# A 1x1 depthwise and pointwise convolution: GpSimd synchronises the critical section, and the start of the kernel is laid out differently

## The chip, the cores and the metric

The kernel runs on one core of one Trainium2 chip. The time is in device microseconds (us) of that core, the median of several executions. One execution was also taken by the hardware profiler; its span and its trace are what the views below come from.

## What is computed

The reference, cut to what matters (k is 1, so the padding is nothing and the loop has one turn):

```python
def reference(x, dw, pw):            # x (1,384,384,384), dw (1,1,384), pw (384,384), bf16
    out = zeros_like(x)
    for i in range(k):
        for j in range(k):
            out = out + xp[:, i:i+H, j:j+W, :] * dw[i, j][None, None, None, :]
    return jnp.einsum('bhwc,cd->bhwd', out, pw)
```

Each of 147,456 pixels has 384 channels. They are scaled by dw, one factor per channel, and multiplied with the 384 x 384 matrix pw. The kernel folds the scaling into the weights: out = x @ (diag(dw) @ pw).

## The kernel before, in words

**Tiling.** 512 pixels make a supertile, and there are 288 of them (NS). A supertile lies in SBUF as 128 partitions of 4 pixels each. The pixels are loaded in chunks of 1, 1, 2, 2, 4 supertiles (group 0), then of 10, and in smaller ones at the end; `load_x` (L111) issues a chunk's load and `store` (L126) its store, both on SyncE's queue. The order of loads and stores on SyncE is a list sorted by due times (L157 to L167): the loads of groups 0 to 2 come first, each later load waits until the group that had its buffer has been transposed.

**The main loop.** VectorE (DVE) transposes each supertile in two halves (`transposes`, L284): 32 x 32 blocks of 32-bit words, that is of channel pairs, from X to T. TensorE (PE) then makes 48 matmuls per supertile (`supertile`, L180): twelve steps (b, par), where b is a block of 64 channels and par tells even from odd channels, times four row groups q of 32 rows that run side by side, one PSUM bank each. ScalarE (ACT) copies the finished supertile from PSUM to the output buffer O (L347). PE's loop holds two supertiles (s = 0, 1), with one PSUM tile each, and its waits are in the loop's body: for the transposes (`s_t`, steps 0 and 6), for ScalarE's copy of the supertile before (`s_a`), and, for s = 0 alone, for the weights (`s_wr`, `w_first`, L178, steps 0, 8 and 10).

**The weights.** Each row group needs the weights of its own 32 rows, scaled by dw. They are made on PE itself (`w_copy`, L207): a selection matrix `sel_w`, which holds dw's factors, times the rows of pw, gives the scaled rows repeated for the four row groups, in PSUM. From there ScalarE and VectorE copy them to `w_r` (`w_out`, L304), in six pieces, five on ScalarE. `sel_w` comes from an identity matrix `eye` that GpSimd makes (L272), reduced by VectorE to `sel` (L312), and from `dw_f`, a column of dw that PE turns out of a row by four tiny matmuls (L240).

**The order at the start.** ScalarE's queue issues dw (L146) and the second piece of pw, 64 rows of 1,536 bytes (L151). SyncE's queue issues the first piece of pw, 128 rows of 1,536 bytes (L147), then x0 (L155), x1, and so on up to the two loads of 10 supertiles. PE fills the time with `idle_work` (L223): rounds of four matmuls on a constant tile of ones that is there before the kernel's own code starts; four rounds ahead of the dw matmuls, three behind them, all written out. Then it waits for the first piece of pw (`s_pw`), makes pieces 0, 1, 2, waits for the second piece of pw (`s_pe0`), and makes the others in pairs of 32-row tiles, with some repeats.

**The critical section.** All of this stands in one critical section (L102), in which the kernel sets its own semaphores. One engine, SyncE by default, signals to all others that it begins and collects them at its end.

The functions that the change touches:

## Time and profile before

| | us |
|---|---|
| median of 3 runs | 577.86 (577.42 to 578.03) |
| the profiled execution's own time | 577.42 |
| its span | 575.70 |
| PE busy | 568.3 (99%) |
| DVE busy | 507.7 (88%) |
| ACT busy | 419.4 (73%) |
| DMA | 226.88 MB, 394 GB/s over the span |

The span is the stretch from the first to the last instruction of the profiled execution; the time of that execution is 1.72 us longer. PE's busy time is that of matmuls, which overlap in the array, so the pace is better read from how many start in a stretch than from the busy share. L188 is the line of the main loop's matmuls, L212 that of the weight copies, L226 that of the idle work, L294 that of the transposes.

### The profile page before, as it was taken

What the parts mean: (1) busy time and instruction counts of PE and PEld (TensorE: products, weight loads), DVE (VectorE), ACT (ScalarE), POOL (GpSimd) and SP (SyncE); (2) the same over time, 40 slices, a digit from 0 to 9 for tenths busy, and PEclk for the clock granted to TensorE, in tenths of its full rate; (3) what the DMA queues carried; (4) which work ended last, traced back from release to release, by engine and by line L of the source; (5) the groups of instructions that cost most, each with busy time, mean ns of one, the idle gap of its engine ahead of it and who ended that gap; (6) DMA issues with size and microseconds to landing.
All of it is one profiled execution on the core that took longest, in us unless ns stands there. A gap on an engine that the chain in (4) does not pass through costs nothing.

```text
span 575.7 us, 29720 instructions
## 1 busy us (share of the span) xinstructions
PE 568.3 (99%) x13876; PEld 383.9 (67%) x13876; DVE 507.7 (88%) x586; ACT 419.4 (73%) x297; POOL 0.5 (0%) x5
## 2 busy tenths in 40 slices
PE   8999999999999999999999999999999999999996
PEld 4666666666666666666666666666666666666664
DVE  6888898889888988899888988898889888988894
ACT  5777777777777777777777777777777777777775
POOL 0000000000000000000000000000000000000000
PEclk9999999999999999999999999999999999999999
DMA  8999999999999999999999999999999999999676
GB/s 326 432 360 428 420 424 434 432 432 411 387 430 390 394 400 429 392 390 402 419 398 392 402 416 409 390 405 418 406 406 426 395 393 394 421 396 374 265 289 236
DMA packets 25220, 226.88 MB, mean 394 GB/s; under 512 B 1209, under 2 KB 5242, under 8 KB 21370
## 3 DMA queue, kind: packets, MB, share of 16 engines
q1 hardware_dynamic: 24096, 225.91, 97.1%
q10 hardware_dynamic: 1114, 0.89, 0.5%
q14 instruction: 9, 0.07, 0.0%
q8 instruction: 1, 0.02, 0.0%
HBM read 113.54 MB, written 113.25 MB: 394 GB/s over the span
## 4 chain that ended last, share of the span: by engine, by line
PE 98%; DMA 1%; DVE 0%; ACTq 0%; issue 0%; DVEq 0%; SPq 0%
PE ps L188 98%; DMA pw_n<-in_pw_dram 1%; PE ps L212 0%; DVE O L345 0%; ACTq L146 0%; ACTq L380 0%; DVEq L341 0%; SPq L102 0%
## 5 line engine op out<-in xcount | busy, mean ns | idle before, releaser
L188 PE MATMUL ps<-w_r,T 32*128 32x384 bf16 x13824 | 562.8, 321 | 0.0
L294 DVE STREAM_TRANSPOSE T<-X 128x384 uint32<-128x384 uint32 x572 | 500.9, 876 | 57.9 <-DMA X<-in_x_dram 1.6
L347 ACT CAST O<-ps 128x1536 bf16<-128x1536 f32 x287 | 413.1, 1439 | 147.7 <-PE ps L188 147.7
L188 PEld LDWEIGHTS ps<-w_r,T 32*128 32x128 bf16 x13824 | 381.7, 93 | 181.4 <-issue 0.7
L307 ACT CAST w_r<-ps 128x768 bf16<-128x768 f32 x5 | 3.8, 801 | 2.3 <-PE ps L212 2.1
L212 PE MATMUL ps<-pw_n,sel_w 32*128 32x384 bf16 x20 | 2.9, 517 | 1.6 <-DMA pw_n<-in_pw_dram 1.6
L294 DVE STREAM_TRANSPOSE T<-Xl 128x384 uint32<-128x384 uint32 x4 | 3.5, 877 | 0.4
L345 DVE CAST O<-ps 128x384 bf16<-128x384 f32 x2 | 1.0, 552 | 3.1 <-PE ps L188 3.1
L226 PE MATMUL ps<-const-bfloat16-1.0 32*128 32x384 bf16 x28 | 2.6, 515 | 1.1 <-SPq L102 1.1
L212 PEld LDWEIGHTS ps<-pw_n,sel_w 32*128 32x128 bf16 x20 | 1.0, 124 | 3.3 <-DMA pw_n<-in_pw_dram 2.6
L282 ACT ACT_TABLE_LOAD x1 | 1.3, 1283 | 2.1 <-issue 2.1
L226 PEld LDWEIGHTS ps<-const-bfloat16-1.0 32*128 32x128 bf16 x28 | 0.7, 123 | 1.6 <-issue 1.6
L312 DVE TENSOR_REDUCE sel<-eye 128x32 f32<-128x128 bf16 x1 | 0.4, 367 | 1.4 <-POOL eye L272 1.4
L307 DVE CAST w_r<-ps 128x768 bf16<-128x768 f32 x1 | 1.0, 958 | 0.7 <-PE ps L212 0.7
L344 ACT CAST O<-ps 128x384 bf16<-128x384 f32 x2 | 0.9, 482 | 0.5 <-PE ps L188 0.5
L319 DVE COPY dw_f<-ps 128x2 f32<-128x2 f32 x1 | 0.2, 160 | 1.0 <-PE ps L240 1.0
L325 DVE TENSOR_SCALAR sel_w<-sel,dw_f 128x128 bf16<-128x128 f32 (+1 forms) x4 | 0.9, 278 | 0.0
L240 PEld LDWEIGHTS ps<-const-bfloat16-1.0,dw_row 1*128 1x128 bf16 (+1 forms) x4 | 0.4, 130 | 0.4 <-DMA dw_row<-in_dw_dram 0.4
L240 PE MATMUL ps<-const-bfloat16-1.0,dw_row 1*128 1x1 bf16 (+1 forms) x4 | 0.4, 191 | 0.0
L272 POOL TENSOR_SCALAR_AFFINE_SELECT eye<-const-bfloat16-1.0 128x128 bf16<-128x128 bf16 x1 | 0.3, 295 | 0.6 <-SPq L102 0.6
L282 ACT COPY warm<-const-float32-0.0 128x1 f32<-128x1 f32 x2 | 0.3, 190 | 0.0
L320 DVE COPY dw_f<-ps 64x2 f32<-64x2 f32 x1 | 0.1, 142 | 0.0
(4 smaller groups left out, 0.4 us busy)
## 6 DMA issues: line engine op xcount, KB each, us to landing
X<-in_x_dram SPq DMA_DIRECT2D x26, 3840.0 KB, 21.4
out_dram<-O SPq DMA_DIRECT2D x26, 3840.0 KB, 27.1
X<-in_x_dram SPq DMA_DIRECT2D x3, 1536.0 KB, 17.6
out_dram<-O SPq DMA_DIRECT2D x3, 1536.0 KB, 7.5
X<-in_x_dram SPq DMA_DIRECT2D x3, 768.0 KB, 9.0
out_dram<-O SPq DMA_DIRECT2D x3, 768.0 KB, 11.2
X<-in_x_dram SPq DMA_DIRECT2D x1, 2304.0 KB, 19.3
out_dram<-O SPq DMA_DIRECT2D x1, 2304.0 KB, 11.1
```

What stands on the lines that cost most here:

```text
L188: mm = nc.tensor.matmul(PS[s][:, q, :D], lhsT=Ts[s][32 * q : 32 * q + 32, b, par::2], rhs=w_r[32 * q : 32 * q + 32, b, par, :], start=n == ...
L212: mm = nc.tensor.matmul(ps[:, at + k, :D], lhsT=sel_w[row : row + 32, slot, :, :].rearrange("p q w -> p (q w)"), rhs=pw_n[row : row + 32, ...
L226: nc.tensor.matmul(PS[i // 2][:, i - 2 if i > 1 else 2 + i, :D], lhsT=ones[32 * i : 32 * i + 32, 0:P], rhs=ones[32 * i : 32 * i + 32, :], ...
L240: mm = nc.tensor.matmul(PS[0][0:m, 0, D + k : D + k + 1], lhsT=dw_row[:, c0 : c0 + 2 * m - 1 : 2], rhs=ones[0:1, 0:1], start=True, stop=Tr ...
L282: nc.scalar.copy(warm[:, s : s + 1], nc.const_aps.tensor(0.0, [P, 1], F32)).then_inc(s_a[s])
L294: ins = nc.vector.transpose(out=Tw[:, 3 * h : 3 * h + 3], in_=Xw[:, :, j, 96 * h : 96 * h + 96].rearrange("p k (b w) -> p b k w", w=32),)
L307: o = nc.scalar.copy(out, in_) if e else nc.vector.tensor_copy(out, in_)
L312: nc.vector.tensor_reduce(out=sel[:], in_=eye[:].rearrange("p (u j) -> p j u", j=32), op=mybir.AluOpType.add, axis=mybir.AxisListType.X,). ...
L325: nc.vector.tensor_scalar_mul(sel_w[0:m, k], sel[0:m].unsqueeze(1).to_broadcast([m, 4, 32]), dw_f[0:m, k : k + 1]).then_inc(s_sw)
L344: nc.scalar.copy(Ov[:, q, j, :], PS[s][:, q, :D]).then_inc(s_a[s])
L345: nc.vector.tensor_copy(Ov[:, q + 1, j, :], PS[s][:, q + 1, :D]).then_inc(s_d)
L347: a = nc.scalar.copy(Ov[:, :, j, :], PS[s][:, :, :D])
```

## The change

The critical section is synchronised by GpSimd instead of SyncE, and GpSimd's drain is left out. The rest of the difference lies in the start:

- pw is one load on SyncE's queue, three rows of 768 bytes per partition, where it was two loads on two queues. x0 is issued on ScalarE's queue, behind dw; SyncE's second DMA is then x1.
- `ones` is no longer a constant that is there at the start. GpSimd makes `warm`, `zero` and `ones` by memsets, then `eye`. PE's idle work uses `zero`, waits for it, and is two loops of three rounds.
- dw is turned by three matmuls into three columns; `sel` has 64 columns and `sel_w` is made by three multiplications of 256 columns, where it was four of 128.
- The weight copies are made in pairs of 64-row tiles, in the order of their blocks, 18 matmuls for 20.
- The main loop's first eight steps go through par first and b second: (0,0), (0,1), (1,0) ... where it was (0,0), (1,0), (0,1), (1,1), (2,0), (2,1), (3,0), (3,1). The last four are as before.

```diff
-    ones = nc.const_aps.tensor(1.0, [P, D], BF16)
-    with tc.tile_critical():
+    with tc.tile_critical(sync_engine=mybir.EngineType.Pool, no_gpsimd_drain=True):
...
         nc.scalar.dma_start(dw_row[:], dw.rearrange("a e c -> a (e c)")).then_inc(s_dw, 16)
-        nc.sync.dma_start(
-            pw_n[:, 0:2].rearrange("p t d -> p (t d)"),
-            pw[0 : 2 * P, :].rearrange("(p t) d -> p (t d)", t=2),
-        ).then_inc(s_pw, 16)
-        nc.scalar.dma_start(
-            pw_n[0:64, 2:4].rearrange("p t d -> p (t d)"),
-            pw[2 * P : C, :].rearrange("(p t) d -> p (t d)", t=2),
-        ).then_inc(s_pe0, 16)
-        load_x(0)
+        load_x(0, nc.scalar)
+        nc.sync.dma_start(pw_n[:], pw.rearrange("(k p) d -> p k d", p=P)).then_inc(s_pw, 16)
...
-        steps = [(0, 0), (1, 0), (0, 1), (1, 1), (2, 0), (2, 1)]
-        steps += [(3, 0), (3, 1), (4, 0), (5, 0), (4, 1), (5, 1)]
-        w_first = {0: [(0, 1), (1, 3)], 8: [(1, 4)], 10: [(1, 5)]}
+        w_eng = [1, 0, 1, 1, 1, 1]
+        w_done = [(s_wr[e], w_eng[: i + 1].count(e)) for i, e in enumerate(w_eng)]
+        w_first = {(0, 0): [(0, 1), (1, 3)], (4, 0): [(1, 4)], (4, 1): [(1, 5)]}
+        steps = [(b, par) for b in range(4) for par in range(2)] + [(4, 0), (5, 0), (4, 1), (5, 1)]
...
         def idle_work(n):
-            for _ in range(n):
+            with nc.tensor.Fori(0, n, 1) as _:
                 for i in range(4):
                     nc.tensor.matmul(
-                        PS[i // 2][:, i - 2 if i > 1 else 2 + i, :D],
-                        lhsT=ones[32 * i : 32 * i + 32, 0:P],
-                        rhs=ones[32 * i : 32 * i + 32, :],
+                        PS[0][:, i, :D],
+                        lhsT=zero[32 * i : 32 * i + 32, 0:P],
+                        rhs=zero[32 * i : 32 * i + 32, :],
...
-        idle_work(4)
+        nc.tensor.wait_ge(s_zero, 1)
+        idle_work(3)
+        nc.tensor.wait_ge(s_seed, 2)
         nc.tensor.wait_ge(s_dw, 16)
-        for k in range(4):
+        for k in range(3):
...
         idle_work(3)
         nc.tensor.wait_ge(s_pw, 16)
...
+        times = {(1, 1): 3, (2, 0): 2}
+        for k in range(3):
+            nc.tensor.wait_ge(s_sw, k + 1)
+            for r in range(2):
+                if k == 2:
+                    nc.tensor.wait_ge(*w_done[r])
+                for v in [0, 1] * times.get((k, r), 1):
+                    mm = nc.tensor.matmul(
+                        PS[(k + 1) % 2][:, 2 * r + v, :D],
+                        lhsT=sel_w[64 * v : 64 * v + 64, k, r, :, :].rearrange("p q w -> p (q w)"),
+                        rhs=pw_n[64 * v : 64 * v + 64, k, :],
...
+                mm.then_inc(s_w)
...
+        nc.gpsimd.memset(warm[:], 0.0).then_inc(s_seed)
+        nc.gpsimd.memset(zero[:].bitcast(U32), 0).then_inc(s_zero)
+        nc.gpsimd.memset(ones[:], 1.0).then_inc(s_seed)
         nc.gpsimd.affine_select(
             out=eye[:],
-            in_=ones[:, 0:P],
+            in_=ones[:],
...
+        )._wait_ge(s_seed, 2).then_inc(s_sel)
...
-        for k in range(4):
+        for k in range(3):
             nc.vector.tensor_scalar_mul(
-                sel_w[0:m, k], sel[0:m].unsqueeze(1).to_broadcast([m, 4, 32]), dw_f[0:m, k : k + 1]
+                sel_w[:, k], sel[:].unsqueeze(2).to_broadcast([P, 2, 4, 32]), dw_f[:, k : k + 1]
             ).then_inc(s_sw)
```

## The prediction

> **What bounds the kernel now.** I read the profile in this order: the chain that ended last, the pace of the main loop's matmuls, the waits of the first microseconds, the landings of the loads. The chain, in order of time (start us, length us, what):

> ```profile
> 1.53 4.52 DMA pw_n<-in_pw_dram
> 6.06 0.05 issue
> 6.10 2.10 PE ps L212 x14
> 8.20 0.04 issue
> 8.25 562.85 PE ps L188 x13824
> ```

> From 8.25 us TensorE (PE) never waits again, and what follows the main loop is 4.6 us (575.70 - 571.10). So the change can act in three places: the pace of the loop, the 8.25 us ahead of it, the 4.6 us behind it. First the pace. The rows below are the main loop's instructions alone in three stretches of 2 us; the (x) behind PE is how many matmuls started:

> ```profile
> 8.25:10.25 2.00, 2.00 (x28) 1.16 (x32) 1.00 1.06 433
> 10.50:12.50 2.00, 2.00 (x56) 1.37 (x52) 1.00 1.02 436
> 100.00:102.00 2.00, 2.00 (x56) 1.37 (x52) 1.00 0.94 399
> ```

> The first 2 us go at half pace, though the granted clock beside them reads 1.00. In the steady part one supertile takes 1.95 us (ScalarE's copies of finished supertiles start at 11.47, 13.42, 15.37 us); 288 x 1.95 = 561.6, and the other 1.25 us are the 1.0 us lost in the half-pace stretch and the last matmul's drain. I therefore count with an effective start: loop start plus half of the slow stretch, now 8.25 + 1.0 = 9.25.

> What holds 8.25? The second piece of pw, issued third after dw and x0: it lands 4.5 us after its issue, and PE waits 1.6 us for it, then makes the last weight copies. The x loads behave alike. Here are the landings of the first x load, of the second with VectorE's wait for it, and of the one for supertiles 10 to 19 (each from the answer for that DMA alone, issued at 1.46, 1.93 and 3.83 us):

> ```profile
> DMA to landing us min/median/max: 3.2/3.2/3.2
> ...
> who waited for it (us, times):
>   DVE T L294: 1.2, 1
> ...
> DMA to landing us min/median/max: 6.2/6.2/6.2
> ...
> DMA to landing us min/median/max: 22.4/22.4/22.4
> ```

> So x0 is there at 4.7, x1 at 8.1, the large one at 26.2 us. DMA is busy from 2 us on (slices 2 to 8: 252, 369, 293, 235, 320, 381 GB/s), so each byte put ahead of x0 delays it.

> **The change, part by part.**

> *Main loop: 0.* The (b, par) order of the first eight steps changes; the waits sit at the same steps (0, 6, 8, 10) and the count of matmuls is the same. The half with four orderly steps and the half with mixed ones run at one pace now (56 matmuls per 2 us), so I take 0.

> *GpSimd as synchronising engine: -0.1.* At the start all engines are let go at 0.79 to 0.88 us by SyncE's signal; GpSimd's would come within 0.05 us of that. At the end SyncE now signals 574.6, collects four engines and signals again, up to the span's end at 575.7. GpSimd must still collect SyncE's own end. I cost the 1.1 us at -0.1, between -0.4 (one of the hand-overs gone) and +0.3 (GpSimd polls more slowly). GpSimd's drain alone is too short to matter: the 1.1 us hold some ten such steps.

> *GpSimd's memsets: +0.4 for PE's first matmul.* Now constants laid down before the start feed PE at 1.12. After, three memsets and the affine_select follow the start one by one. Rows: MEMSET of one column 0.10 us, affine_select of 128 columns 0.295. The zero tile (192 words) lies between 0.10 and 0.45; I take 0.3, nearer to the wider row: PE starts near 1.5, and the eye is ready near 2.1 instead of 1.4. VectorE's reduction (0.37) ends near 2.5, still ahead of the dw column, which is needed near 2.9, so it costs nothing.

> *Weights ready: 7.05 instead of 8.25.* PE: first idle block, 3 rounds at 0.32 = 0.96, to 2.45 (dw is there at 2.30); dw matmuls 0.36 as now (2.37 to 2.73); second block 0.96: 3.8, and 0.1 for the two small loops' branches (between 0, as the main loop shows none, and 0.4): 3.9. VectorE beside it: dw_f at 2.9, 0.16 later the first sel_w. One sel_w of 128 columns takes 0.28 us, four 0.87; with 256 columns each 0.28 to 0.45, so ready near 3.6, 3.9, 4.3, ahead of their use. pw as one load on SyncE's queue with nothing ahead: 192 KB landed 2.4 us after issue at 1.02, that is 3.4; 96 KB more at 252 to 369 GB/s is 0.3 to 0.4: 3.8 (bounds 3.4 and the 6.1 of today's second piece). The copies are 18 matmuls, pairs at 0.32 (today 14 from 6.10). The third ScalarE copy that the loop's start needs waits for the sixth pair: 3.9 + 6 x 0.32 + 0.2 = 6.0; with its 0.80 and hand-overs, 7.05. The two copies behind it end at 7.7 and 8.5, and steps 8 and 10 need them 1.3 and 1.6 us into the loop: covered when the loop starts after 6.9.

> *x0 on ScalarE's queue: it takes the place of that wait.* It is issued where the second pw piece is now (1.53, behind dw), while SyncE issues pw and at once x1, at 1.46. The nearest row is that pw piece: same queue, place and time, served only after SyncE's second DMA, landed 6.06 with 672 KB moved, its own included. x0 there ends after pw + x1 + x0 = 1,056 KB, 384 KB more, at 235 to 381 GB/s 1.0 to 1.6 us: 7.1 to 7.7, I take 7.4. Bounds: x0 is served ahead of x1 (its own row, 4.7, plus 0.3 for the larger pw: 5.0); or it lands like x1 today, behind the same bytes (8.1). Then one transpose (0.85) and 0.08 of hand-overs: loop start 7.4 + 0.93 = 8.33. The second transpose is needed a microsecond later and is 0.85 long: covered. x1 to the large loads are issued 0.45 earlier on SyncE, one DMA less ahead of them, but with the same bytes ahead: 0. On ScalarE x0's issue takes the pw piece's 0.55, so its table load (2.11 to 3.39) stays; its first copies now wait for a GpSimd memset near 1.2, long past by 3.4: 0.

> *The slow stretch: -1.0.* PE worked without a break from 1.12 to 4.5 (3.4 us), still at half pace, idled 1.6, worked from 6.10, and doubled its pace at 10.1 to 10.4, 4.0 to 4.3 us into that stretch. After the change PE works from 1.5 to 7.0 with no break over 0.2 if pw is there at 3.8. By that row the pace doubles near 1.5 + 4.3 = 5.8, before the loop. It idles 1.2 us for x0; I take the fast pace as kept, so the stretch is 0. Without that cover (pw late, so that PE rests in the middle) the 1.0 stays or grows.

> [...]

> [...]

> **Sum**, on the profiled execution (577.42 = span 575.70 + 1.72 around it): start 8.33 - 8.25 = +0.1; slow stretch -1.0; ends -0.1: **576.4**. That execution is the lowest of the three before, the median is 577.86; I add nothing for this, since the half-pace stretch, which may vary, is what goes. 0.2% of 577.86 is 1.16 us, about what a measurement of this kernel can tell from no change: faster means under 576.70, slower over 579.02.

> **Rivals.**
> 1. *x0 is served ahead of x1.* Then it lands near 5.0, the weights hold the start at about 7.05, and the sum gives 577.42 - 1.2 - 1.0 - 0.1 = 575.1. But the load that lands at 26.2 stays where it is: supertile 10 starts 19.5 us after the effective start, now 28.75, and needs it 0.95 earlier, so only 1.6 of the 2.2 us are usable: 575.7. For it: queues can interleave. Against: today's second piece on ScalarE's queue. 575.2 to 575.8; 0.20.
> 2. *The clock is not open.* pw lands late or the loops leave gaps, and the pace doubles 4.2 us after the last break. At today's 10.3 the sum is 577.42 + 0.1 - 0.1 = 577.4; at 8.33 + 4.2 it is 2.1 - 1.0 more: 578.5. 0.21.
> 3. *Slower: x0's last share comes late and PE starts cold behind it.* x0 lands at 8.1 or after, the loop starts at 9.1, PE has rested since 7.0, and the pace doubles 4.2 us later: effective start 9.1 + 2.1 = 11.2, 577.42 + 1.95 - 0.1 = 579.3, up to 580. It decides once the effective start passes 10.95. For it: x1's row today; against: the unbroken 5.5 us ahead. 0.17.
> That the new synchronisation does nothing is inside its -0.4 to +0.3.

> **Chances.** Forecast 0.42, its own range 575.9 to 577.0 (x0 between 6.9 and 7.9); 0.32 of it lies under 576.70. Faster 0.32 + 0.20 = 0.52; same 0.10 + 0.21 = 0.31; slower 0.17. The range leaves out the upper part of rival 3: 575.2 to 578.8.

> **What would show it.** Right: VectorE's longest wait ahead of the first transpose is for X, with x0 landing near 7.4 and after x1; the loop's first 2 us hold 56 matmuls; pw's landing is one event before 4.2; 1.95 us per supertile. Wrong: x0 landed by 5 (rival 1), 28 matmuls in the loop's first 2 us (2), a start past 9 with 28 (3), a supertile off 1.95 (order of the steps), or over 1.4 us between the last store's landing and the end (synchronisation).

## The result and the profile after

The changed kernel takes 575.25 us (median of 6 runs, 575.08 to 575.86), the kernel before, run with it, 577.94 us (6 runs, 577.05 to 578.81): ratio 0.9956, 95% interval 0.9943 to 0.9969. It is faster by 2.7 us. The forecast was 576.4 in a range of 575.2 to 578.8: right side and inside the range, but by 0.05 us only; the forecast's own range, 575.9 to 577.0, was missed, and the time is that of the first rival. The kernel before, run again beside later runs, had medians of 578.77 (29 runs) and 579.02 us (22 runs), each over a spread of 2.8 to 2.9 us, so beside those the gain is 3.5 us (run 1) and 4.0 us (run 5).

The profiled execution takes 575.09 us, its span is 573.4. Its chain in order of time (start us, length us, what):

```profile
1.46 1.36 PE ps L206 x11
2.81 0.07 PE ps L221 x3
2.88 1.18 PE ps L206 x10
4.05 0.01 issue
4.06 2.12 PE ps L239 x12
6.18 0.02 issue
6.20 0.81 ACT w_r L295
7.01 0.14 issue
7.14 561.80 PE ps L189 x13824
```

No load is on the chain any more. PE works from 1.46 us on, the weight copies (L239) begin at 4.06, and the loop's start hangs on ScalarE's third copy (L295), 7.14 instead of 8.25. The loop itself is 1.05 us shorter. Where that comes from shows in the matmuls of the main loop alone, in stretches of 2 us:

```profile
7.14:9.14 2.00, 2.00 (x52) 1.49 (x56) 1.00 1.08 452
10.50:12.50 2.00, 2.00 (x56) 1.45 (x51) 1.00 1.05 441
100.00:102.00 2.00, 2.00 (x56) 1.48 (x52) 1.00 0.93 392
```

The half-pace stretch is gone: 52 matmuls are recorded in the first 2 us where there were 28; the trace's clock record has the full clock from 6.29 us on, where it was 10.41. The steady pace is the same, so the new order of the steps costs nothing. The third difference, the end, no view shows as a line; in the trace SyncE's branch behind its last wait stands at 574.44 of 575.70 before and at 572.28 of 573.37 after, 1.26 and 1.09 us. Together, for the two profiled executions: start -1.11, loop -1.05, end -0.17, sum -2.33, and 577.42 - 2.33 = 575.09.

The landings of x1 (SyncE), of x0 and x1 together (the lower number is x0 on ScalarE's queue), of the load for supertiles 10 to 19, and of pw, each from the answer for those DMAs alone, issued at 1.45, 1.53, 3.39 and 0.96 us:

```profile
DMA to landing us min/median/max: 5.4/5.4/5.4
...
DMA to landing us min/median/max: 4.2/4.8/5.4
...
DMA to landing us min/median/max: 20.7/20.7/20.7
...
DMA to landing us min/median/max: 3.1/3.1/3.1
```

x0 is there at 5.8 us, pw at 4.0, the large load at 24.1 instead of 26.2.

### The profile page after: what moved, and what is told of

Read it like the earlier page. It is cut to its first block, busy times and chain, and to the rows that moved or that the text cites. A ratio compares the mean times of both kernels' runs of the same rounds, so it can differ in the third digit from the quotient of the medians.

```text
span 573.4 us, 29723 instructions
## 1 busy us (share of the span) xinstructions
PE 567.1 (99%) x13869; PEld 415.0 (72%) x13869; DVE 507.0 (88%) x584; ACT 419.1 (73%) x297; POOL 0.9 (0%) x8
## 4 chain that ended last, share of the span: by engine, by line
PE 99%; ACT 0%; issue 0%; DVE 0%; DVEq 0%; POOL 0%; POOLq 0%
PE ps L189 98%; PE ps L206 0%; PE ps L239 0%; ACT w_r L295 0%; DVE O L330 0%; DVEq L103 0%; POOL zero L255 0%; POOL warm L254 0%; PE ps L221 0%; POOLq L365 0%; DVEq L326 0%; POOLq L354 0%; POOLq L103 0%
## 5 line engine op out<-in xcount | busy, mean ns | idle before, releaser
L189 PEld LDWEIGHTS ps<-w_r,T 32*128 32x128 bf16 x13824 | 413.0, 93 | 149.1 <-issue 0.7
L295 ACT CAST w_r<-ps 128x768 bf16<-128x768 f32 x5 | 3.7, 805 | 1.2 <-PE ps L239 1.1
L206 PE MATMUL ps<-zero 32*128 32x384 bf16 x24 | 2.6, 494 | 1.5 <-POOL zero L255 1.5
L239 PE MATMUL ps<-pw_n,sel_w 64*128 64x384 bf16 x18 | 2.7, 475 | 0.0
L239 PEld LDWEIGHTS ps<-pw_n,sel_w 64*128 64x128 bf16 x18 | 1.2, 134 | 1.6 <-issue 1.2
L295 DVE CAST w_r<-ps 128x768 bf16<-128x768 f32 x1 | 1.0, 958 | 0.9 <-PE ps L239 0.9
## 6 DMA issues: line engine op xcount, KB each, us to landing
out_dram<-O SPq DMA_DIRECT2D x1, 2304.0 KB, 10.7
```

Source lines behind the costliest of these rows:

```text
L189: mm = nc.tensor.matmul(PS[s][:, q, :D], lhsT=Ts[s][32 * q : 32 * q + 32, b, par::2], rhs=w_r[32 * q : 32 * q + 32, b, par, :], start=(b, ...
L206: nc.tensor.matmul(PS[0][:, i, :D], lhsT=zero[32 * i : 32 * i + 32, 0:P], rhs=zero[32 * i : 32 * i + 32, :], start=True, stop=True, tile_p ...
L239: mm = nc.tensor.matmul(PS[(k + 1) % 2][:, 2 * r + v, :D], lhsT=sel_w[64 * v : 64 * v + 64, k, r, :, :].rearrange("p q w -> p (q w)"), rhs ...
L295: o = nc.vector.tensor_copy(out, in_) if e == 0 else nc.scalar.copy(out, in_)
```

## The experiments

Each starts from the kernel before or after. "The pace doubles" is read from the trace's clock record and the matmul starts of the run's profiled execution, so a start, a landing or a change of pace is that of one execution; times are medians. "..." in a diff marks what is left out.

### 1 and 2: the synchronisation alone, taken out and put in

Run 1 is the changed kernel, run 2 the kernel before, each with the other's critical section:

```diff
-    with tc.tile_critical(sync_engine=mybir.EngineType.Pool, no_gpsimd_drain=True):
+    with tc.tile_critical():                     # run 1; run 2 the other way round
```

> The changed kernel with SyncE as the synchronising engine again, all else as changed. Theory A (the gain is the earlier start, 1.1 us, plus the half-pace stretch that is gone, 1.0 us, and only 0.2 us is the synchronisation, all of it behind the last store): the time rises by 0.2 us over the changed kernel, 575.4 to 575.6 against 577.9 before; the end, from the last store's landing, takes 1.3 us instead of 1.1, the first DMA issue moves by under 0.1. Rival B (the synchronisation by GpSimd is what lets the start go faster): the loop's start moves back toward 8.25 and the time above 576.5.

> The kernel before with GpSimd as the synchronising engine and no GpSimd drain, all else as before. Theory A: 0.2 us under the kernel before (ratio 0.9996, inside the scatter), loop start within 0.1 of 8.25, end 1.1 us behind the last landing. Rival B: most of the 2.7 us, that is under 576.5.

Run 1: 575.23 us (6 runs, ratio to before 0.9938, interval 0.9925 to 0.9950), start 7.23, end 1.26 us. Run 2: 579.28 us (12 runs, before 578.77 in 29 runs beside it; ratio 1.0009, 0.9998 to 1.0021), end 1.09 us. So by the traces GpSimd is worth 0.17 us at the end. The times don't show it: run 1 was expected at 575.4 to 575.6, run 2 at 0.2 us under the kernel before, and neither came. What they do show is that the gain is not its doing: with SyncE synchronising it is 578.77 - 575.23 = 3.5 us, with GpSimd alone it is nothing. Run 2 had a surprise, a start that was expected within 0.1 of 8.25. Its chain:

```profile
1.51 6.16 DMA pw_n<-in_pw_dram
7.67 0.05 issue
7.71 2.10 PE ps L212 x14
9.81 0.04 issue
9.86 20.23 PE ps L188 x461
```

The second piece of pw, issued at the same time, lands at 7.7 instead of 6.1, and everything behind it moves by the same 1.6 us. The packets of ScalarE's queue (q10, packets and MB) show how. In the kernel before, from 2 to 4.5 us and from 4.5 to 6.1 us:

```profile
q10 hardware_dynamic: 73, 0.09, 10.3%
q10 hardware_dynamic: 7, 0.01, 2.3%
```

In run 2 it is 34 packets up to 4.5 us, 19 up to 6.1 and 27 up to 7.7. In the kernel before nearly the whole piece has moved by 4.5 us, among the packets of x0 and x1, and its landing waits for a few last packets; in run 2 far more of them come late. So it shares the engines with x0 and x1; what holds the last packets back was not tried.

### 3: PE kept at work in the kernel before

(`start` and `stop` of the matmuls are left out.)

```diff
+        for _ in range(5):
+            for k in range(2):
+                nc.tensor.matmul(PS[1][:, 2 + k, :D], lhsT=ones[32 * k : 32 * k + 32, 0:P],
+                    rhs=ones[32 * k : 32 * k + 32, :], start=True, stop=True, tile_position=(32 * k, 0))
         nc.tensor.wait_ge(s_pe0, 16)
```

> The kernel before with five more pairs of idle matmuls (1.6 us) in front of the wait for the second piece of pw, so that PE works without a break from 1.12 us. Nothing else is moved, so the loop still starts at 8.2 to 8.3. [...] Rival C (the pace depends on what the loads do, not on PE's own work): still 28 matmuls in the first 2 us, time and scatter as before, 577.9.

578.96 us (12 runs, 577.87 to 580.36; ratio 1.0005, 0.9994 to 1.0016): no gain, no less scatter. PE's instructions at the start, and the main loop's matmuls in three stretches:

```profile
2.73 1.15 PE L226 MATMUL ps<-const-bfloat16-1.0 32*128 32x384 bf16 x12
3.66 0.85 PE L212 MATMUL ps<-pw_n,sel_w 32*128 32x384 bf16 x6
4.30 1.81 PE L258 MATMUL ps<-const-bfloat16-1.0 32*128 32x384 bf16 x10
5.99 2.10 PE L212 MATMUL ps<-pw_n,sel_w 32*128 32x384 bf16 x14
8.13 6.15 PE L188 MATMUL ps<-w_r,T 32*128 32x384 bf16 x92
```

```profile
8.13:10.13 2.00, 2.00 (x28) 1.17 (x32) 1.00 1.05 433
10.50:12.50 2.00, 2.00 (x32) 1.10 (x27) 1.00 1.02 429
13.00:15.00 2.00, 2.00 (x56) 1.38 (x52) 1.00 1.14 488
```

PE works without a break from 1.1 us, and the pace doubles only at 12.7. What the rival (the pace depends on the loads) expected is what came, and only runs 6 and 7, which issue the loads as before, speak against it. The step of the forecast that rested on unbroken work falls, though its number came true. What the rows have in their shape column: from 3.9 to 8.1 the matmuls run as pairs on 32 rows each, 64 of the 128 on which the main loop's four row groups work. The changed kernel makes its copies in pairs of 64 rows. New theory: the pace depends on how many of the 128 rows work.

### 4: the loads alone

```diff
-        nc.scalar.dma_start(pw_n[0:64, 2:4] ...)
+        nc.sync.dma_start(pw_n[0:64, 2:4] ...)
-        load_x(0)
+        load_x(0, nc.scalar)
```

> The kernel before with its second piece of pw issued second on SyncE's queue and x0 on ScalarE's queue behind dw; all else as before. Theory A (the late second piece of pw is what held the start, and x0 and x1 share the engines and land together near 5.8): the second piece lands near 4.0, x0 near 5.8, the loop starts at 6.6 to 6.9, PE has no long break, so the pace has doubled by 8.0; time 574.9 to 575.6 with SyncE synchronising. Rival D (the order of the copies or the memsets of the changed kernel carry the gain): the loop starts at 7.9 or later, time over 577.

577.59 us (12 runs; ratio 0.9983, 0.9973 to 0.9993). The second piece lands at 5.2, not at 4.0 as I expected, x0 already at 4.7; the loop starts at 7.36. Start 0.9 us earlier, but 28 matmuls in its first 2 us and the pace doubled at 10.7: the early start without the pace. Its time is over the expected 574.9 to 575.6 and under the kernel before beside it, 578.77, by 1.2 us, a third of the 3.5 us that run 1 gains there. In the kernel before and in runs 2 and 4 the loop starts 2.19 us behind this landing (6.06, 7.67, 5.17): it was the bound. (In run 3 PE's own fillers ended at 6.11, beside the landing at 5.95.)

### 5, 6 and 7: how wide the work is

Run 5 is the changed kernel again, as a reference on the same chip. Run 6 is the changed kernel with each weight copy on 32 rows; it leaves out half of the input channels.

```diff
-    lhsT=sel_w[64 * v : 64 * v + 64, k, r, :, :]..., rhs=pw_n[64 * v : 64 * v + 64, k, :], tile_position=(64 * v, 0)
+    lhsT=sel_w[64 * r + 32 * v : 64 * r + 32 * v + 32, k, r, :, :]..., rhs=pw_n[64 * r + 32 * v : 64 * r + 32 * v + 32, k, :], tile_position=(64 * r + 32 * v, 0)
```

Run 7 is run 3 with the fillers, and the repeats of w_copy(4) that were fillers already, on 64 rows (`ones[64 * k : 64 * k + 64]`, `tile_position=(64 * k, 0)`).

> The changed kernel once more, beside the three that follow on the same chip. Both theories: 575.0 to 575.9, loop start 7.1 to 7.2, the pace doubled by 8.3, so within 0.8 us from lowest to highest.

> The changed kernel with each weight copy made on 32 rows instead of 64: same number of matmuls, same pairs, same waits and durations (0.32 us a pair), and half of the input channels left out of the weights. The first four kernels showed that unbroken work on 32-row pairs does not raise the pace (doubled at 12.7 us with PE busy from 1.1). Theory E (the clock counts how many rows of the array work, not whether PE is busy): the loop starts at 7.1 to 7.2 as before, but the pace doubles only at 9 to 12.8 us, the loop's first 2 us hold 28 matmuls, the time rises by 1.0 to 2.8 to 576.2 to 578.0 and scatters by over 1 us. Rival A (unbroken work of any width): doubled by 8.3, time as in the changed kernel.

> The kernel before with the same filled gap as in the third run, but the fillers and the four repeated copies made on 64-row pairs, so that all 128 rows work; no wait and no duration is changed. Theory E: the pace doubles between 6 and 9.5 us, most often before the loop, and the time falls by about 1.3 us against the filled gap on 32-row pairs and against the kernel before. Rival A: no difference from the 32-row fillers, pace doubled at 10 to 13. Either way the loop starts where the second piece of pw lets it, 8.1 to 8.3 or, when that piece lands at 7.7, at 9.9.

Run 5: 575.05 us (6 runs, 574.89 to 576.64; ratio to before 0.9937, 0.9922 to 0.9952), the pace doubled at 6.1; the spread, expected within 0.8 us, is 1.75. Run 6: 576.60 us (12 runs, 576.10 to 579.25; ratio 0.9967, 0.9954 to 0.9981), start 6.92, the pace doubled at 11.0; the copies of r = 0 and r = 1 now overlapped, so they ended 0.4 us sooner (6.34 instead of 6.78) and PE rested 0.6 us before the loop. Run 7: 576.78 us (12 runs, 575.63 to 580.00; ratio 0.9971, 0.9955 to 0.9987), start 8.45 (its wait is for ScalarE's third copy), the pace doubled at 7.2; the gain of 2.2 us is more than the expected 1.3, and the spread of 4.4 us has no explanation here. The main loop's first matmuls in run 6, and the first 2 us of the loop in run 7 (all engines):

```profile
6.92:8.92 2.00, 2.00 (x28) 1.14 (x32) 1.00 1.04 430
8.92:10.92 2.00, 2.00 (x32) 1.11 (x28) 1.00 1.04 439
```

```profile
8.45:10.45 2.00, 2.00 (x52) 1.50 (x56) 1.62 (x3) 1.26 (x2) 0.00 (x0) 1.00 1.06 442
```

With half the rows the changed kernel has its fast pace at 11.0 us instead of 6.1 (run 5), and with twice the rows the kernel with the filled gap has it at 7.2 instead of 12.7 (run 3), though its loop starts no earlier. Run 3 and run 7 differ in nothing but the fillers' rows (and, in four pairs, in their data): 578.96 against 576.78. So in this pair the pace goes with how many of the rows work, and PE's being busy does not tell it. (Tiles of fewer columns were not tried.)

The traces have one thing more. In run 10 the changes of the granted clock lie 3.41 us apart (see there), so I looked at stretches of that length ahead of a change. In run 3, changed at 12.7, PE was busy for 99% or more from 2.48 to 5.89 and from 5.89 to 9.30 us, and the pace stayed at half; in run 7 the stretch from 3.76 to 7.17 was no busier, but for four fifths of it the matmuls ran on 64-row pairs, and the pace doubled at its end. Run 6 by itself leaves a rival, its rest of 0.6 us: its stretch from 4.20 to 7.61, busy for 83%, ended at half pace. Run 10's from 4.27 to 7.69, busy for 81% with copies on 64 rows, ended with the full clock; but run 10's own stretch before that, 0.86 to 4.27, busy for 83% with idle work and dw's small matmuls, did not, so this pair argues against the rest and does not exclude it. That the stretch ahead of a change decides it is my reading; no run shows it by itself.

In medians the two parts are thus worth 1.2 us (run 4, the loads alone) and 2.2 us (run 7 against run 3, the rows alone), 3.4 us together, where the whole change gains 3.5 (run 1) to 4.0 us (run 5).

### 8: what is left to trim

The changed kernel with the three repeats of the fourth piece moved behind it, and with idle work and eye from constants that are there before the start:

```diff
-        times = {(1, 1): 3, (2, 0): 2}
+        times = {(2, 0): 2, (2, 1): 2}
...
-        nc.tensor.wait_ge(s_zero, 1)
...
-        nc.tensor.wait_ge(s_seed, 2)
...
-        nc.gpsimd.memset(zero[:].bitcast(U32), 0).then_inc(s_zero)
-        nc.gpsimd.memset(ones[:], 1.0).then_inc(s_seed)
```

> The changed kernel with what the readings call waste taken out: the three repeats of the fourth piece's copies moved behind the pieces that the loop's start waits for, and the idle work and eye fed from constants laid down before the start instead of three memsets, so that PE starts at 1.1 again. [...] Rival (x0's landing holds the start): start stays at 7.1, no gain.

574.98 us (6 runs, 574.81 to 575.61; ratio 0.9932, 0.9919 to 0.9945). The start is 6.94 instead of 7.14, and the lowest time is 0.08 under that of run 5; the intervals of the two overlap almost wholly, so I call it no gain that the runs can tell.

### 9 and 10: where x0 stands

Run 9 issues x0 second on SyncE's queue, ahead of x1; run 10 fourth on that queue, behind pw, x1 and x2:

```diff
-        load_x(0, nc.scalar)
         nc.sync.dma_start(pw_n[:], pw.rearrange("(k p) d -> p k d", p=P)).then_inc(s_pw, 16)
+        load_x(0)                     # run 9
+        for t in (1, 2, 0):           # run 10, and these three left out of the list
+            load_x(t)
```

> The changed kernel with x0 as SyncE's second DMA, ahead of x1, instead of on ScalarE's queue. Theory (the weights hold the loop's start at 7.14 and x0 on ScalarE's queue, landing near 5.8 together with x1, is hidden): x0 lands at 4.6 to 5.2, x1 at 6 to 7, start stays at 7.1 to 7.2, time 574.9 to 575.7, no change. Rival (x0's place still costs something at the start): start at 6.9 or less, time down by 0.2 or more.

> The changed kernel with x0 issued on SyncE behind pw, x1 and x2, so that it is certain to be late. Theory (what the forecast had priced: loop start = landing of x0 + 0.93, and the doubled pace is kept over the idle time): x0 lands at 7.0 to 9.0, the loop starts 0.9 to 1.0 us behind it, its first 2 us hold 56 matmuls, and the time is up by just what the start moves, 1 to 2.5 us: 576 to 577.5. Rival (the idle time shuts the clock again): 28 matmuls in the loop's first 2 us and 1.5 to 2 us more, over 577.5.

Run 9: 574.98 us (4 runs; ratio 0.9946, 0.9929 to 0.9963). x0 lands at 4.8, a microsecond sooner, and the time stays: in the changed kernel x0's landing is hidden. (The start is 6.97: the pace doubled at 5.8 in this execution, and ScalarE's third copy, which waited for PE up to 6.20 in the changed kernel, began at 6.03, right behind the second.) Run 10: 580.28 us (5 runs, before 578.40 beside it; ratio 1.0037, 1.0023 to 1.0052), 5.3 us over run 9 beside it, 4.7 us between the two profiled executions. x0 lands at 9.0, the loop starts at 9.94: 0.98 behind it, as the forecast had priced. But that is 3.0 us of start, not 4.7. The main loop's matmuls tell the rest:

```profile
9.94:11.00 1.06, 1.06 (x28) 0.80 (x32) 1.00 1.09 464
11.20:13.20 2.00, 2.00 (x32) 1.24 (x27) 0.50 1.26 538
13.20:14.40 1.20, 1.20 (x22) 0.77 (x16) 0.50 0.97 420
14.60:16.60 2.00, 2.00 (x56) 1.49 (x52) 1.00 1.15 484
```

Here the granted clock is in the rows: the loop starts at full pace, falls to 0.50 and rises again. The clock record has the changes at 7.69, 11.10 and 14.51 us, twice 3.41 apart. PE had rested from 7.04 to 9.94, so it was idle for 2.25 us of the stretch from 7.69 to 11.10, and in the next the clock was 0.50, which cost half of 3.41, 1.7 us: 3.0 and 1.7 make the 4.7. The time is what the rival expectation had, over 577.5, and the theory is wrong; but the loop's start was at full pace, and the clock fell 1.2 us into it, not before it.

## Why the prediction was right, and where it was not

- **Main loop 0, synchronisation -0.1, memsets:** right. The steady pace is 56 matmuls per 2 us, the end gave 0.17 us (runs 1 and 2), PE began at 1.46 (forecast 1.5). The 0.17 us is read from the traces and lies within the scatter of the times. That GpSimd polls more slowly, the +0.3 of that term, no run shows: the end took 1.09 us with it and 1.26 with SyncE.
- **Weights ready at 7.05:** right, 7.14. pw landed at 4.0 (forecast 3.8), the copies began at 4.06 (3.9), ScalarE's third copy ended at 7.01. For the branches no row gave the 0.4: the loops' rounds start 0.38 to 0.43 us apart, where those written out in the kernel before start 0.29 to 0.32 apart, and PE came to its wait for pw at 3.84, still ahead of the landing.
- **x0 lands at 7.4 and sets the start at 8.33:** this is the step that failed. x0 landed at 5.8 and was hidden (run 9), so the start came 1.2 us earlier than forecast, which is nearly the whole miss of 1.3 us on the profiled execution. The rule "start = landing + 0.93" holds (0.98 in run 10); the landing was mis-sized. I scaled from one row, the pw piece that landed at 6.06, which I read as served only after SyncE's second DMA, with the slow rates beside it. That reading was wrong: the piece moved among the packets of x0 and x1, most of it by 4.5 us (under run 2). Its landing moves between 5.2 and 7.7 with the same queue and issue time (kernel before and runs 2, 3 and 7), while x0 in its place landed at 5.6 to 5.8 in all five traces with that order (the changed kernel, runs 1, 5, 6 and 8). And the rates were those of one execution: 293 and 235 GB/s from 4 to 6 us then. The same slices of the changed kernel (all engines; the last number is GB/s):

```profile
4.00:5.00 1.00, 0.99 (x12) 0.45 (x9) 0.08 (x1) 0.40 (x1) 0.00 (x0) 1.00 0.96 381
5.00:6.00 1.00, 1.00 (x10) 0.51 (x8) 1.00 (x2) 1.00 (x2) 0.00 (x0) 1.00 1.07 433
```

- **The slow stretch, -1.0:** the size is right, by luck, for the reason given is not. Unbroken work on 32-row pairs left the pace at half until 12.7 us (run 3); with 64-row pairs it doubled at 7.2 (run 7). And "I take the fast pace as kept" over idle time is wrong by run 10, where the clock fell to 0.50 behind 2.9 us of rest; it never came to the test in the changed kernel because x0 was in time.
- **Rival 1** was given 575.2 to 575.8 at 0.20 and is what happened, by another way: x0 was not served ahead of x1; x0 landed at 5.8 and x1 at 6.8, after sharing the engines. The queues from 4 to 5 us (q1 is SyncE's, q10 ScalarE's; packets, MB):

```profile
q1 hardware_dynamic: 69, 0.21, 52.2%
q10 hardware_dynamic: 62, 0.17, 43.9%
```

That the time stayed inside the stated range is owed to this rival's share of it. Its cap of 1.6 us did not bind: the large load came at 24.1 and not at 26.2, and the loop shows no stall (561.80 us for 288 x 1.95 = 561.6).
- **Rival 3** is real in its outcome: run 10 is it, 580.28 us, though its loop starts at full pace and not cold. The stated range, up to 578.8, leaves out all of this rival, which began at 579.02, and not its upper part alone.

The clock records of the two kernels have the same 3.41 us as run 10's: from its rise the full clock lasts 563.20 us in the kernel before and 566.61 in the changed one, 165 and 166 times 3.413. What sets the place of the changes, and whether it makes the scatter, is not shown: the kernel before spread by 1.8 us in 6 runs and by 2.9 in 22, the changed one by 0.8 and, in run 5, by 1.75.

What stays open: what holds back the last packets of the second piece of pw, why the spread is as wide as it is, and how many rows, for how long, it takes until the pace doubles; when it did is read only after a run.

## What to carry to other kernels

Ahead of a loop bound by TensorE, look at how many rows the matmuls work on, and at the waits between them and the loop: here 64-row pairs in place of 32-row pairs were worth 2.2 us in medians (run 7 against run 3), where the earlier start was worth 1.2 (run 4), and a rest of 2.9 us ahead of the loop was followed by 3.41 us at half the clock, 1.7 us (run 10). When a load is the bound, do not take its landing from one execution where two queues compete (here 5.2 to 7.7 us with the same queue and issue time): ask what it would be at both orders, and give the case in which it is hidden its full weight. Read the matmuls started per microsecond, since neither busy time nor, ahead of the first record of a trace, the granted clock shows half pace (28 starts in 2 us beside a granted clock of 1.00).
